# DRAIN instructions on GpSimd in the expert loop of an attention and mixture-of-experts kernel

## The chip, the cores and the metric

The kernel runs on one core of a Trainium2 chip. A core has a matrix engine (TensorE, PE in the profile; PEld is its weight load), VectorE (DVE), ScalarE (ACT), GpSimd (POOL) and a sync engine (SP) that issues most DMAs. Each engine runs its own queue of instructions, and they wait for each other by semaphores. A `q` behind an engine's name (POOLq, SPq) marks instructions of its sequencer: waits, branches, drains, DMA issues. They aren't counted as busy time. The metric is the device time in microseconds, as the median of the runs.

## The reference

Linear attention over 8 batches of 576 tokens with 8 heads of 64, and then a mixture of 8 experts in which each of the 4608 tokens goes to one expert:

```python
kv = np.einsum('bhsd,bhde->bhse', q_s, np.einsum('bhsd,bhse->bhde', k_s, v))   # q_s, k_s: softmaxes
x = attn_out.transpose(0, 2, 1, 3).reshape(B * S, H * D)                       # 4608 x 512
expert_idx = np.argmax(x @ w_gate, axis=1)
for e in range(E):                                                             # 8 experts, F = 1024
    h = np.maximum(x_sorted[lo:hi] @ w1[e], 0.0)
    y_sorted[lo:hi] = h @ w2[e]
return gate_w[:, None] * y
```

## The kernel before, in words

The first part, up to about 165 us, is a hand-ordered schedule over all engines: attention for eight batches, the choice of an expert for each token, and a count of tokens per expert. GpSimd scatters the finished token rows (with their gate value and their token number in two more columns) into a buffer `xs` in DRAM, sorted by expert, 128 rows to a scatter. This is `put`, line 603, 36 scatters: 34 of them in the schedule, and two (the last tokens of the last batch) kept back in the list `behind` and issued at the start of the second part.

The second part is the function `experts`. A table built on the chip says which steps there are; every engine walks it in a loop of its own (`x.walk(body)`), here 14 times, after a start that is written out. A step takes up to 384 sorted tokens in up to three tiles of 128 (`kind` is the number of tiles):

- TensorE multiplies by `w1` (line 994, into `pt` and `ph`) and by `w2` (line 1010, one output tile `py` for each 128 tokens), with both factors split into a high and a low half, three products each.
- ScalarE makes the high half of the hidden values (line 1124), the high half of the next tokens (1120), and scales the output tile by the gate into `yt` (line 1115).
- VectorE makes the low halves (1194 for the hidden values, 1188 for the next tokens), turns the next tokens (1183), and copies gate and token number into `gs` (1190). It waits for the index copy of the step, `sIX`, before it starts 1188 and overwrites `gs`.
- GpSimd copies the token numbers of a step into the index tile `ix` (line 1273) and scatters each `yt` tile into the output by these numbers (line 1262).
- The sync engine loads the next tokens and the next expert's weights.

GpSimd's queue in a step, in order: a table value is read; a wait for `sGS` (the token numbers are there); three waits for `sO`, the landings of the scatters of the step before, since these still read `ix`; the copy; a wait for it; and for each tile a wait for `yt` and a scatter that adds 16 to `sO[u]` once it has landed. `hold` is a semaphore instruction that waits, and does nothing else of use. Ahead of the loop stand the two scatters of `behind` and the three scatters of the first step. The sync engine waits for the landing of the former (`sPU`) before it reads their rows.

Behind the loops ScalarE waits for the last landings (line 1173), and generated instructions end the program. They stand under the lines 920 (closing of the pools) and 1370 (end of the whole program). There each engine executes a DRAIN, GpSimd too; the sync engine waits for each in turn.

Of the kernel before, what the change touches and what calls it, by code (L numbers as in the profile page):

```python
# [924 lines left out]
def experts(nc, tc, g):  # L925
# [324 lines left out]
    def pool():  # L1250
        x = Eng(nc.gpsimd, "pool")
        e = nc.gpsimd
        it = x.reg("it", 1)
        cu = [x.reg(f"c{u}", 2) for u in range(3)]
        du = [x.reg(f"d{u}", 16) for u in range(3)]

        def hold(sem, val, then=sSp):
            e.sem_inc(then, 1).wait_op(sem, val, GE)

        def send(u, again=True):  # L1260
            hold(sYT[u], cu[u])
            e.indirect_dma_start(out=g.out, out_offset=bass.IndirectOffsetOnAxis(ap=g.IX[:, u:u + 1], axis=0), in_=g.YT[u],  # L1262
                                 in_offset=None, bounds_check=N - 1, oob_is_err=False).then_inc(sO[u], 16)
            x.add(f"c{u}", 1)
            if again:
                x.add(f"d{u}", 16)

        def body(j):
            kind = x.get(KD, j, 0, 3)
            hold(sGS, it)  # L1270
            for u in range(3):
                hold(sO[u], du[u])
            e.tensor_copy(g.IX, g.GS[:, :, 1]).then_inc(sIX, 1)
            hold(sIX, it)
            x.add("it", 1)
            send(0)
            with e.If(kind > 1):
                send(1)
            with e.If(kind > 2):
                send(2)  # L1280

        for put in g.late.behind:
            put(sPU)
        for u in range(3):
            send(u, False)
        x.walk(body)

    def sp():
# [69 lines left out]
    act()  # L1358
    dve()
    pool()  # L1360
    sp()

# [30 lines left out]
```

## Time and profile before

| what | value |
|---|---|
| median of 3 runs | 603.73 us (600.47 to 605.41) |
| the profiled execution | 602.93 us, of which the span of instructions is 600.8 us |
| TensorE busy in the span | 560.0 us (93%) |
| VectorE, ScalarE, GpSimd busy | 332.2, 255.4, 127.1 us |
| chain that ended last, share of the span | TensorE 78%, VectorE 8%, DMA 6%, GpSimd 1% |

The times of all views count from the span's start. The chain that ended last is followed back from the last instruction; the rest of the 602.93 us lies outside the span.

### The profile page before, as it was taken

Reading aid. Unit: us, or ns where it says so; the run is one execution under the profiler, and the core shown is the slowest. Engines: PE = TensorE matmul, PEld = TensorE weight load, DVE = VectorE, ACT = ScalarE, POOL = GpSimd, SP = SyncE. Lnnn points to the kernel's source line nnn. Section 1 sums busy time; section 2 is a strip of 40 time slices with the busy share of each in tenths; the row PEclk is TensorE's granted clock in tenths of the full one; section 3 lists DMA queues with packets and bytes.
Section 4 is the critical chain, followed back from the end, with each engine's and each line's share of the span. In section 5 each row is a group of like instructions: output and inputs, shape, how many; then the busy total and the mean of one; then the engine's idle time right before and its main releaser. Section 6 shows DMA issues by size and latency. Waiting matters only on the chain.

```text
span 600.8 us, 11397 instructions
## 1 busy us (share of the span) xinstructions
PE 560.0 (93%) x3787; PEld 499.1 (83%) x3788; DVE 332.2 (55%) x690; ACT 255.4 (43%) x510; POOL 127.1 (21%) x211
## 2 busy tenths in 40 slices
PE   4888888878999999999999999999999999999993
PEld 2577777767978989898998989989898999889892
DVE  5989999995762332636141324274526644482651
ACT  0889888745412222433131213244323615242451
POOL 4122638783511010010102010111001110110100
PEclk9999989996999999999999999999999999999997
DMA  8989998676358730074204020306421470361000
GB/s 270 331 279 338 300 316 286 235 252 224 124 186 261 231 89 17 17 227 142 85 0 105 0 70 19 89 17 198 172 57 53 169 227 0 83 245 48 17 22 5
DMA packets 64719, 87.19 MB, mean 145 GB/s; under 512 B 8623, under 2 KB 50095, under 8 KB 64048
## 3 DMA queue, kind: packets, MB, share of 16 engines
q1 hardware_dynamic: 58112, 66.70, 35.9%
q0 software_dynamic: 6000, 19.03, 8.3%
q10 hardware_dynamic: 576, 1.07, 0.5%
q8 instruction: 18, 0.29, 0.2%
q14 instruction: 13, 0.11, 0.1%
HBM read 64.82 MB, written 22.74 MB: 146 GB/s over the span
## 4 chain that ended last, share of the span: by engine, by line
PE 78%; DVE 8%; DMA 6%; ACT 2%; SPq 2%; issue 1%; POOL 1%; DVEq 0%; POOLq 0%; ACTq 0%
PE py L1010 33%; PE pt L994 17%; PE ph L994 17%; DMA qt<-in_q 5%; PE py L1029 3%; PE ph L710 2%; PE xp L484 2%; DVE kt L329 2%; DMA vs<-in_v 2%; DVE qm L425 1%; DVE xr L503 1%; DVE own L367 1%; PE qT L470 1%; PE kv L357 1%; SPq L171 1%
## 5 line engine op out<-in xcount | busy, mean ns | idle before, releaser
L1010 PE MATMUL py<-w2h,hid 128*128 128x512 f32 x576 | 179.8, 389 | 0.0
L1010 PEld LDWEIGHTS py<-w2h,hid 128*128 128x128 f32 x576 | 108.1, 188 | 22.2
L1010 PE MATMUL py<-w2l,hid 128*128 128x512 f32 x288 | 112.2, 390 | 0.0
L1194 DVE SCALAR_TENSOR_TENSOR hid<-pt,hid 128x384 fp32r<-128x384 f32 x56 | 31.1, 556 | 145.7 <-ACT hid L1124 145.7
L1262 POOL DMA_INDIRECT out<-yt,ix x39 | 39.2, 1004 | 321.4 <-ACT yt L1115 321.4
L1115 ACT ACTIVATE yt<-py,ga 128x512 f32<-128x512 f32 x39 | 26.8, 687 | 142.4 <-PE py L1010 134.1
L1010 PEld LDWEIGHTS py<-w2l,hid 128*128 128x128 f32 x288 | 54.1, 188 | 10.8
L1194 DVE SCALAR_TENSOR_TENSOR hid<-ph,hid 128x384 fp32r<-128x384 f32 x56 | 31.2, 557 | 55.3 <-ACT hid L1124 55.2
L1124 ACT ACTIVATE hid<-ph 128x384 fp32r<-128x384 f32 x56 | 27.5, 491 | 62.1 <-PE ph L994 62.1
L1124 ACT ACTIVATE hid<-pt 128x384 fp32r<-128x384 f32 x56 | 27.4, 490 | 62.0 <-PE pt L994 60.2
L1183 DVE STREAM_TRANSPOSE xx<-xb 128x1536 f32<-128x1536 f32 x14 | 40.7, 2907 | 7.7 <-DVE gs L1190 5.0
L994 PE MATMUL pt<-xh,w1h 128*128 128x384 f32 (+3 forms) x224 | 42.6, 312 | 0.2
L994 PE MATMUL ph<-xh,w1h 128*128 128x384 f32 (+3 forms) x224 | 42.4, 311 | 0.0
L994 PE MATMUL ph<-xh,w1l 128*128 128x384 f32 (+3 forms) x224 | 42.4, 311 | 0.0
L994 PE MATMUL pt<-xl,w1h 128*128 128x384 f32 (+3 forms) x224 | 42.4, 311 | 0.0
L994 PE MATMUL pt<-xh,w1l 128*128 128x384 f32 (+3 forms) x224 | 42.4, 311 | 0.0
L994 PE MATMUL ph<-xl,w1h 128*128 128x384 f32 (+3 forms) x224 | 42.4, 311 | 0.0
L603 POOL DMA_INDIRECT xs<-xr,posi x36 | 35.9, 997 | 30.1 <-issue 12.9
L484 PE MATMUL xp<-kx,qTs 128*128 128x146 f32 x256 | 39.4, 299 | 1.7 <-ACT qTs L477 0.8
L484 PEld LDWEIGHTS xp<-kx,qTs 128*128 128x128 f32 x256 | 34.6, 194 | 3.9 <-ACT qTs L477 1.0
L994 PEld LDWEIGHTS pt<-xh,w1h 128*128 128x128 f32 x224 | 35.9, 189 | 2.0 <-issue 1.0
L994 PEld LDWEIGHTS pt<-xl,w1h 128*128 128x128 f32 x224 | 35.7, 189 | 0.0
(227 smaller groups left out, 909.2 us busy)
## 6 DMA issues: line engine op xcount, KB each, us to landing
raw<-in_moe_w SPq DMA_DIRECT2D x10, 2048.0 KB, 8.3
kt<-in_k SPq DMA_DIRECT2D x14, 640.0 KB, 7.5
xb<-xs SPq DMA_DIRECT2D x32, 192.0 KB
qt<-in_q SPq DMA_DIRECT2D x8, 640.0 KB, 5.3
vs<-in_v SPq DMA_DIRECT2D x8, 640.0 KB, 8.8
qt<-in_q SPq DMA_DIRECT2D x8, 512.0 KB, 6.9
vs<-in_v SPq DMA_DIRECT2D x8, 512.0 KB, 8.9
xt<-in_moe_w SPq DMA_DIRECT2D x8, 256.0 KB, 6.3
```

The lines of the kernel that those rows point to most:

```text
L329: TT(t, t, m[:, :, None, :].to_broadcast([P, 2, SLOT, D]), op=ALU.subtract)
L484: nc.tensor.matmul(xv[:, c, :KW], o.qT[i][:, c, :], kx[:, c, :], start=True, stop=True)
L603: s = nc.gpsimd.indirect_dma_start(out=xs, out_offset=bass.IndirectOffsetOnAxis(ap=n.pi[:, t - t0:t - t0 + 1], axis=0), in_=xr[:, t, :], i ...
L710: m = nc.tensor.matmul(ph, wt[:, c, f * P:(f + 1) * P], xt[:, c, :], start=(n == 0), stop=(n == 3 * NC - 1))
L994: m = e.matmul(ph, wt[:, c, f * P:(f + 1) * P], xt[:, c, :w], start=(n == 0), stop=(n == 3 * NC - 1))
L1010: m = e.matmul(g.PY[u], ht[:, f, u * P:(u + 1) * P], wt[:, f, :], start=(n == 0), stop=(n == 3 * NF - 1))
L1029: m = e.matmul(g.PY[u], ht[:, f, u * P:(u + 1) * P], wt[:, f, :], start=(n == 0), stop=(n == 3 * NF - 1))
L1115: m = e.activation(g.YT[u], g.PY[u], AF.Copy, scale=g.GA[:, u:u + 1]).wait_op(sPY[u], cu[u], GE)
L1124: e.activation(g.HH[:, f, :], g.PH[f][:, :W], AF.Relu).wait_op(sPH[f], it, GE).then_inc(sHH[f], 1)
L1183: e.transpose(g.XX, g.XB.rearrange("p t (a c) -> p c t a", c=NC)).wait_op(sB, b80, GE)
L1194: e.scalar_tensor_tensor(g.HL[:, f, :], g.PH[f][:, :W], 0.0, g.HH[:, f, :].bitcast(F32), op0=ALU.max, op1=ALU.subtract).wait_op(sHH[f], it ...
L1262: e.indirect_dma_start(out=g.out, out_offset=bass.IndirectOffsetOnAxis(ap=g.IX[:, u:u + 1], axis=0), in_=g.YT[u], in_offset=None, bounds_c ...
```

## The change

One DRAIN is put at the head of GpSimd's step, behind the table read and ahead of the waits, and one behind the two scatters of `behind`, ahead of the first step's output scatters. No instruction is taken out or moved, and no other engine's program is changed. The DRAIN in the generated end of the program stays.

```diff
         def body(j):
             kind = x.get(KD, j, 0, 3)
+            e.drain()
             hold(sGS, it)
             for u in range(3):
                 hold(sO[u], du[u])
...
         for put in g.late.behind:
             put(sPU)
+        e.drain()
         for u in range(3):
             send(u, False)
         x.walk(body)
```

## Rows read from the trace of the kernel before

**Rows 1.** The page, chain that ended last: shares of the span by engine.

```profile
PE 78%; DVE 8%; DMA 6%; ACT 2%; SPq 2%; issue 1%; POOL 1%; DVEq 0%; POOLq 0%; ACTq 0%
```

**Rows 2.** Stretches: length, busy us (instructions) of PE, PEld, DVE, ACT, POOL; clock, DMA.

```profile
190.00:350.00 160.00, 160.00 (x820) 146.68 (x819) 60.78 (x83) 44.45 (x77) 15.36 (x20) 1.00 0.32 98
350.00:593.00 243.00, 240.25 (x1406) 217.85 (x1404) 118.84 (x163) 95.16 (x161) 26.44 (x33) 1.00 0.29 92
...
594.20:599.20 5.00, 0.00 (x0) 0.00 (x0) 0.00 (x0) 0.00 (x0) 0.00 (x0) 0.50 0.00 0
```

**Rows 3.** Line 920, 585 to 601: durations in ns min/median/max, first and last start.

```profile
L920 DVEq DRAIN  x1: 1074/1074/1074, 588.4 to 588.4; - x1
L920 POOLq DRAIN  x1: 6839/6839/6839, 592.4 to 592.4; - x1
L920 PEldq DRAIN  x1: 8/8/8, 594.2 to 594.2; - x1
L920 ACTq DRAIN  x1: 8/8/8, 594.7 to 594.7; - x1
```

**Rows 4.** Line 1173: ScalarE's waits for the last landings.

```profile
L1173 ACTq EVENT_SEMAPHORE  x3: 17/17/17, 594.5 to 594.6; - x3
```

**Rows 5.** DMA: issues from 592 to 601 (us to landing); packets 594.2 to 599.2.

```profile
out<-yt,ix POOLq DMA_INDIRECT x1, 2.4
...
DMA packets 0, 0.00 MB, mean 0 GB/s; under 512 B 0, under 2 KB 0, under 8 KB 0
```

**Rows 6.** Waits of the sync engine, 585 to 601: total us, times, longest.

```profile
SPq L920 <- POOLq L920: 4.5, 1, 4.5
...
SPq L920 <- ACTq L920: 0.5, 1, 0.5
```

**Rows 7.** Lines 1370 and 1379: drains and the clearing of semaphores on GpSimd.

```profile
L1370 POOLq DRAIN  x3: 34/41/212, 599.3 to 600.5; - x3
L1370 POOLq EVENT_SEMAPHORE_RANGE_CLEAR  x1: 589/589/589, 599.9 to 599.9; - x1
...
L1379 POOLq DRAIN  x1: 198/198/198, 0.3 to 0.3; - x1
```

**Rows 8.** Lines 603 and 1262: GpSimd's scatters, and from issue to landing (line 603).

```profile
L603 POOL DMA_INDIRECT xs<-xr,posi x36: 956/972/1553, 72.9 to 170.8; - x36
DMA to landing us min/median/max: 2.7/5.1/7.5
...
L1262 POOL DMA_INDIRECT out<-yt,ix x39: 966/978/2082, 182.7 to 592.1; - x39
```

**Rows 9.** Timeline of GpSimd, VectorE, TensorE: start, length, what, idle before and releaser.

```profile
170.85 0.96 POOL L603 DMA_INDIRECT xs<-xr,posi  x1 [0.31 <-issue]
182.68 1.00 POOL L1262 DMA_INDIRECT out<-yt,ix  x1 [10.87 <-ACT yt L1115]
...
421.68 0.51 POOL L1273 CAST ix<-gs 128x3 int32<-128x3 f32 x1 [7.70 <-DMA out<-yt,ix]
425.71 1.76 DVE L1188 TENSOR_TENSOR xl<-xx,xh 128x1536 fp32r<-128x1536 f32 x1 [0.68 <-ACT xh L1120]
434.00 0.81 PE L994 MATMUL pt<-xh,w1h 128*128 128x352 f32 x4
...
530.47 0.60 POOL L1273 CAST ix<-gs 128x3 int32<-128x3 f32 x1 [7.28 <-DMA out<-yt,ix]
534.60 1.76 DVE L1188 TENSOR_TENSOR xl<-xx,xh 128x1536 fp32r<-128x1536 f32 x1 [0.69 <-ACT xh L1120]
...
577.55 0.18 POOL L1273 CAST ix<-gs 128x3 int32<-128x3 f32 x1 [1.48 <-DMA out<-yt,ix]
592.09 0.98 POOL L1262 DMA_INDIRECT out<-yt,ix  x1 [14.35 <-ACT yt L1115]
```

**Rows 10.** Waits of GpSimd over the span: total us, times, longest.

```profile
POOL out L1262 <- ACT yt L1115: 321.4, 39, 19.1
POOL ix L1273 <- DMA out<-yt,ix: 57.0, 14, 7.8
```

## The prediction

> **What bounds the kernel now.** I read the page's chain that ended last first. It puts 78% of the span on TensorE (PE in the rows) and 1% on GpSimd (POOL) [rows 1]. The table of stretches says why: from 190 to 350 us TensorE is busy in all 160.00 us, and from 350 to 593 us in 240.25 of 243. In the 5.00 us from 594.2 to 599.2 every engine stands at 0.00 [rows 2]. So there are two places to look at. In the expert steps a drain on GpSimd matters only if it reaches TensorE. Behind the last matmul there is a tail in which nothing computes, and a microsecond there is a microsecond of the result.
>
> **The tail** is read from the views of the lines under which the generated instructions of the start (L1379), of the pools' closing (L920) and of the end (L1370) stand. The last scatter is issued at 592.09 for 0.98 us and lands 2.4 us after its issue [rows 5, 9]; ScalarE's three waits on the scatters' semaphores go through from 594.5 to 594.6, and its drain runs at 594.7 [rows 3, 4]. GpSimd's own DRAIN starts at 592.4 and takes 6.839 us, so it ends at 592.4 + 6.84 = 599.24 [rows 3]. Between 594.2 and 599.2 the DMA view counts no packet [rows 5]. The drain therefore goes on for about 4.7 us after the last scatter has landed, with no data moving. The sync engine's waits price this: it waits 4.5 us for that drain, beside 0.5 us for ScalarE's [rows 6]. What then follows (three more drains of 34 to 212 ns on GpSimd, a clearing of semaphores of 589 ns) ends the span at 600.8 and is not touched [rows 7].
>
> **What the drain does for 4.7 us.** The drains around it separate the candidates. GpSimd's three drains after 599.3, with nothing issued since the one before, cost 0.03 to 0.21 us [rows 7]; those of TensorE's and ScalarE's queues cost 8 ns, and VectorE's 1.07 us, begun at 588.4 while its last instructions still ran [rows 3]. So a drain as such is cheap, and waiting for the engine's own work explains only the part up to 593.07, where the last scatter's instruction ends. What this one has and the others lack is a history. Before it these lines show on GpSimd only the 198 ns drain at the start of the program [rows 7], and the kernel calls none itself, while 36 + 39 = 75 scatters went out [rows 8]. I read it as a cost per scatter issued since the last drain: an estimate of (599.24 - 594.5) / 75 = 63 ns each if the count begins at the landing, (599.24 - 593.07) / 75 = 82 ns each if it begins where the scatter's instruction ends. That is inferred, not shown, since the trace holds only one drain behind a scatter.
>
> A rule of the Trainium skill speaks against a gain. The Trainium skill, VectorE: DVE Perf Modes, section "The DRAIN you can't avoid", calls the drains of the preamble and postamble a constant of about 12 ns on all five engines; by it neither the added nor the last drain is worth anything and the time stays where it is. The 8 ns rows agree with it, GpSimd's 6.839 us doesn't [rows 3]. The Trainium skill, PSUM — Partial Sum Buffer, section "Engine vs sequencer instructions", has a drain wait until the engine is fully idle; by it alone the drain would end at 593.07 and not at 599.24.
>
> **The change part by part.** Nothing is removed and nothing changes its order; 14 + 1 DRAINs are added to one queue (14 is the count of the index copies, one in each step [rows 10]).
>
> (1) The drain behind the two left-over scatters. The second is issued at 170.85 and ends at 171.81 [rows 9]. The longest landing of this kind is 7.5 us [rows 8], so all data is down by 170.85 + 7.5 = 178.4. By my reading 36 scatters cost 36 x 0.082 = 3.0 us, behind the landing at worst: 181.4. GpSimd's next work, the first output scatter, waits for a ScalarE result until 182.68 [rows 9]. Cost 0. If it were late, the next to wait would be ScalarE's write of the same buffer one step later.
>
> (2) The drain in a step, ahead of the waits. Behind it on the queue stand the waits for the gate copy and for the three scatters' landings, then the index copy (L1273), then the next scatters. If the drain needs the landings, so do the waits right behind it: GpSimd stands 57.0 us over 14 copies for just that [rows 10]. The extra is what comes after the landing: at least 0.03 us (a drain with nothing to do), for three scatters 3 x 0.082 + 0.21 = 0.46 us. The far bound is the whole measured excess of 4.7 us at each drain. Who waits for the copy: VectorE, before it makes the low half of the next tokens (L1188), which TensorE needs at the start of the next step. The tightest steps are those where expert weights load beside the scatter. In the one at 421.68 the copy ends at 421.68 + 0.51 = 422.19, VectorE starts L1188 at 425.71 (held by ScalarE) and ends it at 427.47, TensorE needs it at 434.00 [rows 9]. That gives 3.5 us free before VectorE notices, and 3.5 + 6.5 = 10.0 us before TensorE does. The steps with copies at 476 and 530 repeat the pattern; in the latter 534.60 - 531.07 = 3.5 us is free before VectorE notices [rows 9]. Both 0.46 and 4.7 are under 10.0: cost 0 at either end. The scatters that follow the copy wait for ScalarE's results anyway, 321.4 us in 39 waits [rows 10].
>
> (3) What stays for the last drain. The last step's drain stands before its copy at 577.55, and after it comes one scatter, at 592.09 [rows 9]. So one scatter's share instead of 75: the drain ends at the landing, 594.5, plus 0.08, or plus 0.21 if it costs as much as the dearest idle one. The sync engine has ScalarE's drain behind it by 594.8, so the whole wait of 4.5 us [rows 6] goes, less at most 0.2. I take 4.4.
>
> **Sum.** The profiled execution took 602.93 us (span 600.8): 602.93 + 0 + 0 - 4.4 = 598.5. The median of the runs shown is 603.73, 0.8 above it, which gives 599.3. I forecast 599.0, between the two. The four times shown lie between 600.47 and 605.41, a spread as wide as the gain.
>
> **Rivals.**
> - *The last drain costs the same whatever went before* (something fixed that GpSimd does at a drain behind any scatter). For it: a single such drain can't tell a share per scatter from a fixed 4.7 us. Against it: nothing moves or computes in that time, and idle drains are at 0.03 to 0.21 us. Then the step drains cost 4.7 us each, hidden under the 10.0, and the time stays at 603 to 603.7. The constant drain of the Trainium skill (VectorE: DVE Perf Modes, same section) ends here too. Chance 0.17.
> - *Only a part goes*: a fixed share of 1 to 3.5 us and a smaller one per scatter. Time 600 to 602.5. Chance 0.08.
> - *Slower*: the step drains reach TensorE. Place: the three steps with 10.0 us of room. Price: three times what a drain lasts over 10.0 us beyond the landing. It decides from 10.0 us on, and for 1% (6 us) needs 12 us a drain. The longest drain in the trace is 6.84 us in all, its excess 4.7, so it would have to be more than twice as long. With 12 us, 602.93 + 6 - 4.4 = 604.5 if the tail still shrinks, 609 if not. Chance 0.03.
> - *The forecast*: the wait at the end goes. Chance 0.72.
>
> **How the numbers follow.** Under the forecast the spread of the runs, moved by 4.4, is 596.1 to 601.0; that is the forecast's own range. The rivals with less or no gain lie from 600 to 605.4. Taking in the smaller gain and most of the no-gain case I end at 604.0, and at 595.5 below for a somewhat quicker set of runs. About 1% is what a measurement of this kernel can tell from no change. 1% is 6.0 us, more than the 4.5 that the tail can give at most; it needs luck in the scatter of the runs: faster 0.12. Slower by over 1% is the slow rival alone: 0.03. The rest, 0.85, is within 1%.
>
> **What would show it.** Right: GpSimd's last DRAIN is at 2.2 to 2.5 us instead of 6.84; the sync engine's wait for it falls from 4.5 to under 0.3; the span ends some 6.3 us after the last scatter's landing minus 4.4, so about 1.9 to 2; the step drains end within 0.5 us of the landing; the drain behind the left-over scatters takes longer than the landing alone explains; the index copies move by less than 0.5 us, and the chain still runs through TensorE in every step. Wrong: a last drain near 6.8 us again, with step drains that run some 4.7 us past their landings (the fixed cost); or L1188 held by GpSimd's copy and TensorE idle at the start of a step. The weakest step is the reading of the 4.7 us as a cost per scatter.

## The result, and the profile after

The changed kernel takes 597.57 us in the median (594.03 to 602.74, 18 runs) against 603.55 us before (600.47 to 605.97, 18 runs). The ratio is 0.9904, with a 95% interval from 0.9883 to 0.9925. Two further timings of the same kernel, each beside runs of the kernel before on its own chip, gave 0.9947 (0.9921 to 0.9972) and 0.9928 (0.9902 to 0.9954). The profiled execution is at 598.12 us with a span of 595.9 us, 4.9 us below the span before.

The end of the program comes first. The view of line 920 of the changed kernel has durations in ns (min/median/max) and the first and last start; with it come the drains on GpSimd under line 1372 (1370 before) and ScalarE's waits for the last landings.

```profile
L920 DVEq DRAIN  x1: 1072/1072/1072, 588.0 to 588.0; - x1
L920 POOLq DRAIN  x1: 2111/2111/2111, 592.1 to 592.1; - x1
L920 PEldq DRAIN  x1: 8/8/8, 593.8 to 593.8; - x1
L920 ACTq DRAIN  x1: 8/8/8, 594.4 to 594.4; - x1
...
L1372 POOLq DRAIN  x3: 46/53/212, 594.2 to 595.7; - x3
...
L1173 ACTq EVENT_SEMAPHORE  x3: 17/17/17, 594.1 to 594.3; - x3
```

GpSimd's last drain went from 6839 to 2111 ns [rows 3] and now ends at 592.1 + 2.1 = 594.2, with the landing at 594.1. The span ends 1.8 us behind the landing. The drains of the other engines are as they were. What the sync engine waits for from 585 to 601 us (total us, times, longest):

```profile
SPq L920 <- PEq L920: 21.5, 1, 21.5
SPq L1372 <- PEq L1372: 1.2, 2, 1.0
SPq L920 <- ACTq L920: 0.5, 1, 0.5
```

The row of 4.5 us for GpSimd [rows 6] is gone; ScalarE's 0.5 us is now the last. From the start of the last scatter to the end of the span there were 600.8 - 592.09 = 8.7 us, and there are 595.9 - 591.71 = 4.2: 4.5 us of the 4.9 lie here.

Then the added drains (lines 1270 and 1285), and the timeline of GpSimd around them (start, length, what, idle before and releaser):

```profile
L1285 POOLq DRAIN  x1: 8117/8117/8117, 169.5 to 169.5; - x1
...
L1270 POOLq DRAIN  x14: 1723/2434/8174, 196.1 to 575.5; - x14
```

```profile
170.49 0.96 POOL L603 DMA_INDIRECT xs<-xr,posi  x1 [0.30 <-issue]
182.35 1.00 POOL L1262 DMA_INDIRECT out<-yt,ix  x1 [10.90 <-ACT yt L1115]
...
421.53 0.30 POOL L1274 CAST ix<-gs 128x3 int32<-128x3 f32 x1 [7.93 <-DMA out<-yt,ix]
...
577.64 0.74 POOL L1274 CAST ix<-gs 128x3 int32<-128x3 f32 x1 [1.95 <-DMA out<-yt,ix]
591.71 0.98 POOL L1262 DMA_INDIRECT out<-yt,ix  x1 [13.33 <-ACT yt L1115]
```

The step drains are not short: 2.4 us in the middle, 8.2 at most. Yet nearly all of it is the landing that the waits behind them stood for before. The copy of the last step comes 1.95 us after the last scatter's instruction, where it came 1.48 us after it [rows 9]. Over all 14 copies GpSimd's wait rose from 57.0 us [rows 10] to 61.1, 0.3 us a step in the mean, while the scatters that follow waited less for ScalarE, 313.0 us instead of 321.4. GpSimd's waits (total us, times, longest):

```profile
POOL out L1262 <- ACT yt L1115: 313.0, 39, 18.6
POOL ix L1274 <- DMA out<-yt,ix: 61.1, 14, 8.4
```

TensorE doesn't see any of it. From 190 to 350 us it is busy throughout, as before [rows 2], and from 350 to 590 us for 239.76 us in both kernels. The columns are length of the stretch, busy us (instructions) of PE, PEld, DVE, ACT and POOL, TensorE's clock, DMA share and GB/s. The first two rows are the changed kernel, the third is the kernel before:

```profile
190.00:350.00 160.00, 160.00 (x819) 146.73 (x818) 60.44 (x83) 44.54 (x76) 16.73 (x20) 1.00 0.31 97
350.00:590.00 240.00, 239.76 (x1404) 217.51 (x1403) 118.73 (x163) 94.53 (x160) 28.37 (x31) 1.00 0.29 93
```

```profile
350.00:590.00 240.00, 239.76 (x1405) 217.79 (x1404) 118.84 (x163) 94.47 (x160) 25.52 (x32) 1.00 0.29 93
```

The other 0.4 us of the profiled difference are older than the first added drain: the second left-over scatter is at 170.49 instead of 170.85 [rows 9], and no instruction up to there has changed. From that scatter to the last one it is 592.09 - 170.85 = 421.24 us before and 591.71 - 170.49 = 421.22 after: the added drains cost nothing in between.

### The profile page after: what moved, and what is told of

It reads as the page before. It is cut to its first block, busy times and chain, and to the rows that moved or that the text cites. A ratio compares the mean times of both kernels' runs of the same rounds, so it can differ in the third digit from the quotient of the medians.

```text
span 595.9 us, 11412 instructions
## 1 busy us (share of the span) xinstructions
PE 560.8 (94%) x3787; PEld 500.3 (84%) x3788; DVE 332.2 (56%) x690; ACT 255.7 (43%) x510; POOL 131.8 (22%) x211
## 4 chain that ended last, share of the span: by engine, by line
PE 79%; DVE 9%; DMA 5%; ACT 2%; issue 2%; SPq 1%; POOL 1%; POOLq 0%; DVEq 0%; ACTq 0%
PE py L1010 33%; PE pt L994 17%; PE ph L994 17%; DMA qt<-in_q 4%; PE py L1029 3%; PE xp L484 2%; PE ph L710 2%; DMA vs<-in_v 2%; DVE kt L329 2%; DVE qm L425 1%; DVE xr L503 1%; PE qT L470 1%; DVE own L367 1%; PE kv L357 1%; ACT qs L444 1%
## 5 line engine op out<-in xcount | busy, mean ns | idle before, releaser
L1262 POOL DMA_INDIRECT out<-yt,ix x39 | 43.5, 1117 | 313.0 <-ACT yt L1115 313.0
```

## The experiments

The theory was that a drain on GpSimd pays for each scatter issued since the drain before it. The rivals were a cost of the last drain that stays whatever went before, and a cost that any earlier drain takes away whole. The kernels below are the kernel before with other drains, unless said otherwise. All compute the whole result.

**A drain behind the loop, right ahead of the last one.**

```diff
         x.walk(body)
+        e.drain()
```

> One drain behind the loop, right ahead of the one that ends the program. Theory: the added drain takes 6.8 us for its 75 scatters and the last one under 0.3 us; the sum in the tail and the time stay, ratio 0.999 to 1.001. If the long time belonged to the last drain itself, wherever others stand, the added one takes 2.1 us, the last one still 4.7 us. If each drain with a scatter in flight before it cost a fixed 4.7 us and idle ones nothing, it looks as in the theory, and the other runs of this set tell.

Measured: 0.9998 (0.9975 to 1.0021). The added drain (line 1287), the last one, and the sync engine's wait:

```profile
L1287 POOLq DRAIN  x1: 6857/6857/6857, 597.3 to 597.3; - x1
...
L920 POOLq DRAIN  x1: 41/41/41, 604.2 to 604.2; - x1
```

```profile
SPq L920 <- POOLq L920: 4.6, 1, 4.6
```

The whole cost moved to the added drain and the last one is left with 41 ns. So it isn't tied to the instruction that ends the program; whoever drains first pays, and a drain without cover pays in the open. A fixed cost of any drain behind a scatter would look the same here; the next runs tell the two apart.

**One drain alone, behind the two left-over scatters.**

```diff
         for put in g.late.behind:
             put(sPU)
+        e.drain()
```

> One drain alone, the one behind the two left-over scatters; none in the steps. Theory (the last drain pays for each scatter issued since the drain before it): 36 scatters are paid there and 39 are left, so the last drain lasts 2.11 + 38 x 0.064 = 4.5 us (0.064 = (6.84 - 2.11) / 74, from the kernels before and after) and the time falls by 2.3 us, ratio 0.996. Rival, all or nothing (any earlier drain takes the whole cost away): last drain 2.1 us, time down by 4.7 us or more, ratio 0.990 to 0.992. Rival, fixed cost: last drain 6.8 us, ratio 1.000.

Measured: 0.9962 (0.9941 to 0.9984). The last drain is at 3889 ns and the sync engine waits 1.6 us for it. That is between the 6.8 of a fixed cost and the 2.1 of a cost taken away whole, so both rivals fall; it is also 0.6 us under the 4.5 expected, so one price per scatter beyond the landing isn't right either. The last drain (line 920) and the sync engine's wait for it:

```profile
L920 POOLq DRAIN  x1: 3889/3889/3889, 599.0 to 599.0; - x1
```

```profile
SPq L920 <- POOLq L920: 1.6, 1, 1.6
```

**Drains in the first steps only,** so that 16, 24 or 6 scatters are left for the last drain (the bound is 8, 5 and 12).

```diff
             kind = x.get(KD, j, 0, 3)
+            with e.If(j < 8):
+                e.drain()
             hold(sGS, it)
```

> Drains in the first eight steps only. Behind the eighth drain 2+3+2+3+2+3+1 = 16 scatters are issued. Theory: last drain 2.11 + 15 x 0.064 = 3.1 us, time down by 3.8 us, ratio 0.994. All or nothing: last drain 2.1 us, ratio 0.990 to 0.992. Fixed cost of the last drain: 6.8 us, ratio 1.000.

> Drains in the first five steps; 3+2+3+2+3+2+3+2+3+1 = 24 scatters are left for the last drain. One price of 0.083 us from the end of the last scatter's instruction (0.67 us after the drain's start): 0.67 + 24 x 0.083 = 2.66 us. With 16 left it was 2.73 instead of max(2.1, 0.67 + 16 x 0.083 = 2.0). If a part of the count comes behind the landing, this one too is above its 2.66, near 3.1 to 3.4.

> Drains in the first twelve steps; 2+3+1 = 6 scatters are left. One price that runs beside the landing: 2.1 us, the landing alone. If a part of the count comes behind the landing: 2.2 to 2.5 us.

Measured for eight steps: ratio 0.992 (0.9892 to 0.9947). The three last drains, for eight, five and twelve steps:

```profile
L920 POOLq DRAIN  x1: 2727/2727/2727, 596.7 to 596.7; - x1
```

```profile
L920 POOLq DRAIN  x1: 3054/3054/3054, 595.1 to 595.1; - x1
```

```profile
L920 POOLq DRAIN  x1: 2331/2331/2331, 592.7 to 592.7; - x1
```

With 6, 16 and 24 scatters they lie 0.22, 0.62 and 0.94 us over the 2.11 us of a single one: 41 to 44 ns for each further scatter (0.22/5, 0.62/15, 0.94/23). Five and twelve steps were run once each, for the profile. The price that runs wholly beside the landing (2.1, 2.1 and 2.66 us) is refuted.

**The cost without a landing in it:** a drain ahead of the two left-over scatters, and one in the last step behind its waits, where everything issued before has landed.

```diff
+        e.drain()
         for put in g.late.behind:
             put(sPU)
...
             for u in range(3):
                 hold(sO[u], du[u])
+            with e.If(kind < 2):
+                e.drain()
```

> Two drains, each where everything issued before it has landed: one ahead of the two left-over scatters (34 scatters into xs behind it) and one in the last step, behind its waits for the landings (2 scatters into xs and 38 into the output). Their lengths are then the drain's own cost with no landing in it. The last drains so far stood over the landing by 0.0, 0.6, 1.8 and 4.7 us for 1, 16, 39 and 75 scatters, which is not one price. Theory A, two prices (0.082 us for a scatter into xs, 0.045 for one into the output): first 34 x 0.082 = 2.8 us, second 2 x 0.082 + 38 x 0.045 = 1.9 us. Theory B, one price that runs beside the landing of the last scatter (0.082 us each from the drain's start): first 2.8 us, second 40 x 0.082 = 3.3 us. Theory C, a price that grows with the count: first under 1.8 us, second about 1.9 us. By all of them the last drain is 2.1 us.

Measured: the two drains (lines 1284 and 1274) have lengths that are their own cost.

```profile
L1274 POOLq DRAIN  x1: 3326/3326/3326, 578.7 to 578.7; - x1
...
L1284 POOLq DRAIN  x1: 2843/2843/2843, 170.0 to 170.0; - x1
```

2843 / 34 = 84 ns and 3326 / 40 = 83 ns. Both kinds of scatter cost the same, so two prices (A) and a price that grows with the count (C) fall; one price (B) had 2.8 and 3.3 us. The two drains also tell the scatters from GpSimd's other work and from time. The rows show the stretches ahead of each drain, with the columns of the result:

```profile
0.00:170.00 170.00, 137.77 (x1458) 115.80 (x1460) 142.43 (x388) 110.99 (x266) 82.54 (x156) 0.96 0.78 262
172.90:578.70 405.80, 405.65 (x2230) 368.49 (x2229) 176.67 (x253) 135.47 (x229) 44.08 (x53) 1.00 0.34 104
```

GpSimd executed 156 counted instructions in the 170 us ahead of the first drain and 53 in the 405.8 us ahead of the second. The lengths go as 34 to 40, the scatters, and not as either of these. All scatters have 128 rows, so a price for each row can't be told from one for each scatter. Together with the 41 ns behind the landing this gives a fit with two halves. A first count of 41 ns a scatter starts where the last scatter's instruction ends, 0.67 us after the drain's start in the tail; a second of 41 ns a scatter starts when the first is through and the last scatter has landed, 2.07 us after the drain's start:

| scatters since the last drain | fit: max(0.67 + 0.041 n, 2.07) + 0.041 n | measured, us |
|---|---|---|
| 1 (all fifteen drains) | 2.11 | 2.11 |
| 6 | 2.32 | 2.33 |
| 16 | 2.73 | 2.73 |
| 24 | 3.05 | 3.05 |
| 39 | 3.87 | 3.89 |
| 75 (before) | 6.82 | 6.84 |

The fit was made after these runs; for the two drains with everything landed it gives 2.79 and 3.28 us, 0.05 us too little each. That there are two passes inside the drain is a reading of it; the trace has one row for a drain.

**One drain alone, in the last step,** timed twice, the second time beside the changed kernel.

```diff
             kind = x.get(KD, j, 0, 3)
+            with e.If(kind < 2):
+                e.drain()
             hold(sGS, it)
```

> One drain alone, in the last step (the only one with a single tile). Theory: it pays for 74 scatters, so it runs some 4.7 us past the landing of the scatters and the index copy of this step starts near 582 instead of 577.6, still about 9 us ahead of the scatter that needs it; the last drain is 2.1 us as with all fifteen, and the time falls by 4.7 us, ratio 0.992. If the fifteen drains together brought more than the tail (the timed gain was 6.0 us, the tail's 4.7), this one falls short of them by 1.3 us. Fixed cost: last drain 6.8 us, ratio 1.000.

> One drain alone, in the last step. Theory: ratio 0.992, the same as after_third within 0.2%.

> The changed kernel beside the one with a single drain, on one chip. Theory: both lose the same 4.7 us at the end and nothing else, ratio 0.992, and differ by less than 0.2%. If fifteen drains bring more than one, this is lower than last_step_again by the 1.3 us between the first timings (0.2%).

> The changed kernel once more, beside the others on one chip. The tail alone gives 4.7 us, ratio 0.992; the first timing gave 6.0 us, 0.9904. If fifteen drains bring more than the one in the last step did (0.9933), this stays at 0.990 or below; if the difference was the scatter of the runs, it comes out at 0.991 to 0.993.

Measured for the single drain: 0.9933 (0.9907 to 0.9958) and 0.9916 (0.9889 to 0.9944); for all fifteen 0.9928 in the same set as the latter, and 0.9947 in the set before. The last of these lies above the 0.991 to 0.993 expected for scatter alone; its interval reaches down to 0.9921. From the first of these four: the drain, the last drain, and the copy behind the former in GpSimd's timeline.

```profile
L1271 POOLq DRAIN  x1: 6307/6307/6307, 581.4 to 581.4; - x1
...
L920 POOLq DRAIN  x1: 2118/2118/2118, 597.9 to 597.9; - x1
```

```profile
580.60 0.97 POOL L1262 DMA_INDIRECT out<-yt,ix  x1 [4.47 <-ACT yt L1115]
588.17 0.19 POOL L1275 CAST ix<-gs 128x3 int32<-128x3 f32 x1 [6.59 <-issue]
597.60 0.98 POOL L1262 DMA_INDIRECT out<-yt,ix  x1 [9.25 <-ACT yt L1115]
```

It pays 6.3 us for its 74 scatters, the copy waits that long, and the scatter behind still has 9.25 us to wait for ScalarE. One drain does what fifteen do as far as these runs tell: in the one set that has both it is 0.9916 against 0.9928, the other way round than the first timings of different sets (0.9933 against 0.9904). The excess that the first timing seemed to have over the tail did not come again.

**How much lateness the steps take.** The changed kernel with a GpSimd memset of a tile of its own ahead of each index copy (14000 columns here, 7000 in the other).

```diff
+            e.memset(g.PAD, 0.0)
             e.tensor_copy(g.IX, g.GS[:, :, 1]).then_inc(sIX, 1)
```

> The changed kernel, and in each step a GpSimd memset of 7000 columns of bf16 ahead of the index copy, some 3.5 to 7 us long. The room found in the trace of before (10.0 us between the copy and the need of TensorE in the three tightest steps) covers it: no change against the changed kernel, ratio to the kernel before 0.990 to 0.992. If the room is smaller than 7 us, it loses three times the difference.

> The same with 14000 columns, some 7 to 14 us. With 14 us the copy of the three tight steps comes about 4 us behind the room of 10.0: TensorE stands about 4 us at the start of the step behind each, and the last scatter is issued about 1 us later: 3 x 4 + 1 = 13 us more than the changed kernel, ratio to the kernel before about 1.013. With a memset of only 7 us nothing changes, ratio 0.990 to 0.992.

Measured: 0.9942 (0.9919 to 0.9965) with 5.93 us a step, 0.9919 (0.9892 to 0.9947) with 11.77 us a step. The changed kernel without a memset was at 0.9947 in the same set, so neither loses anything that can be told from it. From the kernel with 11.77 us: VectorE's waits for the copy (total us, times, longest), then one of the three tight steps, and VectorE's work ahead of it, in the timelines of GpSimd, the sync engine, VectorE and TensorE.

```profile
DVE xl L1189 <- POOL ix L1276: 34.5, 11, 4.4
```

```profile
396.20 1.76 DVE L1189 TENSOR_TENSOR xl<-xx,xh 128x1536 fp32r<-128x1536 f32 x1 [3.31 <-POOL ix L1276]
...
405.38 0.13 DVE L1185 TENSOR_TENSOR gn<-xg,ep 128x6 f32<-128x6 f32 x1
...
409.74 0.97 POOL L1263 DMA_INDIRECT out<-yt,ix  x1 [4.46 <-ACT yt L1116]
...
412.58 0.36 SPq L1331 DMA_DIRECT2D raw<-in_moe_w  x1
...
412.91 11.77 POOL L1275 MEMSET pad<- 128x14000 bf16 x1 [2.20 <-DMA out<-yt,ix]
...
424.92 1.76 DVE L1189 TENSOR_TENSOR xl<-xx,xh 128x1536 fp32r<-128x1536 f32 x1 [3.51 <-POOL ix L1276]
...
430.39 0.81 PE L995 MATMUL pt<-xh,w1h 128*128 128x352 f32 x4
```

The same step in the changed kernel, and then in the kernel with 5.93 us:

```profile
405.77 0.12 DVE L1184 TENSOR_TENSOR gn<-xg,ep 128x6 f32<-128x6 f32 x1
...
412.63 0.97 POOL L1262 DMA_INDIRECT out<-yt,ix  x1 [4.46 <-ACT yt L1115]
...
413.00 0.37 SPq L1329 DMA_DIRECT2D raw<-in_moe_w  x1
```

```profile
411.60 0.97 POOL L1263 DMA_INDIRECT out<-yt,ix  x1 [4.45 <-ACT yt L1116]
...
411.94 0.36 SPq L1331 DMA_DIRECT2D raw<-in_moe_w  x1
...
420.70 5.93 POOL L1275 MEMSET pad<- 128x7000 bf16 x1 [8.13 <-DMA out<-yt,ix]
```

VectorE does wait for the copy now, in 11 steps, but it is done with the low half at 424.92 + 1.76 = 426.68, 3.7 us ahead of TensorE's need. The 13 us expected did not come, for two reasons: the memset was 11.77 us and not 14, and the scatter no longer lands late. The expert's weights are issued 2.8 us after the scatter (412.58 against 409.74), where in the changed kernel it was 0.4 us (413.00 against 412.63), and the wait ahead of the memset is 2.20 us instead of the 7.93 ahead of the copy. So the memset ends 412.91 + 11.77 - 409.74 = 14.9 us after the scatter's start, where the copy stood 421.53 - 412.63 = 8.9 us after it: the copy of this step is 6.0 us later, not 11.77. With the 3.7 us left, that is 9.7 of the 10.0 us of room. A lateness beyond the room was not reached, so the 10.0 us are a reading of the trace and not a measured edge.

Why the load moved can be followed in the trace. In both kernels it is issued 7.2 us after VectorE starts the last part of its turn of the next tokens (412.58 - 405.38 and 413.00 - 405.77), and with the long memset VectorE had stood 3.31 us for the copy of the step before. That the load is what makes the scatter land late is argued: with 5.93 us the load is still 0.3 us behind the scatter, and the wait is 8.13 us.

## Why the prediction was right, point by point

- **Where to look.** A drain could matter in the tail or through TensorE; it mattered in the tail alone, by 4.5 us of the 4.9 between the profiled spans.
- **What the 4.7 us were.** The step called weakest, a cost per scatter issued since the last drain, holds: the last drain follows the count in six kernels, and the cost moves to whichever drain comes first (the drain behind the loop, 6857 and 41 ns). Of the two estimates, 63 and 82 ns, the one that counts from the end of the scatter's instruction is right: 83 to 84 ns with everything landed. What it left out is that half of it can't begin before the landing. For 75 scatters this changes nothing; for 39 and fewer it does, and the expectations worked out with 64 ns beyond the landing were off by up to 0.6 us (4.5 against 3.89).
- **The drain behind the left-over scatters (1), cost 0.** It ran from 169.5 to 177.6, inside the worst case of 181.4, and the first output scatter still waits for ScalarE.
- **The step drains (2), cost 0.** The extra was put at 0.03 to 0.46 us a step; it is 0.3 us in the mean and 0.47 in the last step. The cover named for it, 10.0 us in the tightest steps, was enough: with the long memset the copy of one such step came 6.0 us later and left 3.7 us ahead of TensorE's need. The copies moved a little more than the 0.5 us named as a sign: in one step the copy stood 269.89 - 261.08 = 8.81 us behind the scatter ahead of it, and now 270.11 - 260.73 = 9.38.
- **What stays for the last drain (3).** 2.2 to 2.5 us were expected and 2.11 measured, just below; the sync engine's wait of 4.5 us is gone whole.
- **The sum.** 4.4 us were taken, at most 4.5 to be had. The first timing shows 603.55 - 597.57 = 6.0 us, and its interval (0.9883 to 0.9925, so 4.5 to 7.1 us) holds the tail's 4.5 only at its edge. The two later ones show 0.9947 and 0.9928, 3.2 and 4.3 us by 603 us. All three intervals hold 0.9922 to 0.9925, the 4.5 to 4.7 us of the tail. No view shows a second gain, and the single drain in the last step does as well, so the excess of the first timing is scatter as far as these runs tell: it brought the first ratio near the 1% that was called luck. About 1% was also taken as the least that a measurement can tell; the intervals here reach 0.2 to 0.3% to either side.
- **The rivals.** The fixed cost fell with the changed kernel, whose last drain follows one scatter and takes 2.11 us, and with the single drain behind the left-over scatters (3.89 us). The drain behind the loop alone would not have refuted it. The constant drain of the Trainium skill (VectorE: DVE Perf Modes, section "The DRAIN you can't avoid") fell too: that page's figure, given for the drains that the runtime adds, is near those of TensorE, ScalarE and the sync engine (7 to 13 ns here) and far from one on GpSimd that follows scatters. That only a part goes fell as well: nothing of the 4.7 us past the landing is left but 0.1. The slow rival needed 12 us a drain; the longest drain of all these kernels that pays for a full count alone, 74 or 75 scatters, is 6.3 to 6.9 us in all.

## What to carry to other kernels

Look at the end of the program for an engine that works on although nothing moves and nothing computes: here the sync engine's waits showed 4.5 us behind the last landing. On GpSimd a DRAIN cost 83 ns here for each scatter of 128 rows issued since the drain before it, and behind the one that ends the program there is no work to hide it. So issue one late in the kernel, where GpSimd waits anyway and the work behind it has room for the whole count (one with 74 scatters took 6.3 us and was covered); more drains added nothing here, and one placed in the tail only moves the cost.

## What the runs showed of the hardware that was not expected

- The drain's cost has two halves, by the fit. 41 ns a scatter can run beside the last landing, 41 ns a scatter come behind it: 6, 16 and 24 scatters put it at 2.33, 2.73 and 3.05 us, where the landing alone would have covered a single pass of 6 or 16.
- Scatters that have long landed are paid like those in flight: 34 of them cost 2.84 us, though their last packets had moved 3 us before the drain began.
- How long a scatter takes to land goes with how close behind it a weight load starts: in one step GpSimd waits 7.93 and 8.13 us with the load 0.4 and 0.3 us behind the scatter, and 2.20 us with the load 2.8 us behind. No run moves the load alone.
